# Per-head q and k transfers, a searched order of the engines, and last rows stored in two halves, in a fused attention and maxout-FFN kernel

## The chip, the core and the metric

The kernel runs on one NeuronCore of a Trainium2 chip. The core has five instruction queues that run side by side[...]: TensorE (PE in the profile; its weight loads are listed apart as PEld), VectorE (DVE), ScalarE (ACT), GpSimd (POOL) and SyncE (SP). Sixteen DMA engines move data between memory and the on-chip SBUF; a transfer is started by an instruction on POOL, SP or ACT. The metric is the device time of one execution in microseconds, taken as a median over runs.

## The reference

Batch 4, 8 heads, 768 positions, head width 64, in float32. Each query attends to the 128 latest positions and to the first 4 positions ("sinks"). The result goes through a feed-forward layer with three up-projections of which the largest value is kept:

```
scores = (q @ k.T) / sqrt(64)
keep   = (col < 4) | ((0 <= row - col) & (row - col < 128))
a      = softmax(where(keep, scores, -1e9))
x      = (a @ v)            # heads side by side: 3072 rows x 512
h      = max(x @ w1, x @ w2, x @ w3)      # 3072 x 768
out    = h @ w_out                        # 3072 x 512, float32
```

## The kernel before

**Tiling.** The 3072 rows are 24 tiles of 128. Two tiles make a chunk of 256 positions, three chunks make a batch, so chunks 0 to 11 cover the four batches. The eight heads are two groups (g = 0, 1) of four, and four heads lie on the four 32-partition quarters of a tile. One unit of attention is a chunk and a group: scores for four heads on PE (line 484), exponential on ACT (490), mask on DVE (498), product with v on PE (516, and 507 for the sinks), reciprocal and scaling on DVE (526, 535). The scaled rows are then turned so that features lie on partitions: in the first five blocks by PE and a copy on ACT (545, 565), from block 5 (`FIRST_BY_DMA`) on by a DMA transpose that SP issues (570).

**Blocks.** The feed-forward layer runs over blocks of two or four tiles, listed in `BLOCKS`: 2, 2, 2, 4, 4, 4, 4, 2 tiles. Per block there are 18 up-projection groups of four matmuls each (643, called H below, of 256 columns in a block of two tiles and 512 in one of four), evacuated by ACT (652) and by DVE with a running maximum (657), and for each tile one output group of six matmuls with the matrix `wo` (671, called Y), copied by ACT (678) and stored by SP (685). The attention of a later block runs beside the feed-forward work of an earlier one.

**Transfers.** q and k are loaded by POOL with a cast to bf16 (198): one transfer for q or k, a chunk and a group, over 128 partitions of 512 elements. v is loaded per tile over all heads (204), the three up-projection matrices in nine transfers of two column blocks each (209: w0, w2, w4 below, three transfers each), and `wo` in one (310). Only the very first q, and the first k of group 1, come in float32 on SP and ACT (188) and are cast by ACT (349); the first k of group 0 comes on POOL. The chunk's q and k are then transposed on DVE (345). POOL may have eight loads under way: each waits for the one eight places before it, and POOL's loads are kept in the order in which they are listed: first k, v of chunk 0, q and k of chunk 1, v of chunk 1, w0, w2, w4, q and k of chunk 2, its v, `wo`, then chunk by chunk. The cast buffers of q and k hold eight chunks, so chunk 8 waits until chunk 0's have been transposed.

**Order.** No engine chooses its order at run time. The program builds a list of tasks, each with an engine, a cost in microseconds, what it depends on, and a due time `want`; `arrange` plays them through a model of the engines, the PSUM and SBUF rings and one DMA server (0.38 MB per us, 0.2 for v), and at each step takes what can start first, with ties going to the earlier `want`. The order in which it took them is the order in each engine's queue. An instruction whose input is late holds up everything behind it on its engine.

Of the kernel before, what the change touches and what calls it, by code (L numbers as in the profile page):

```python
# [40 lines left out]
def arrange(tasks):  # L41


    engines = {}
    for n, t in enumerate(tasks):
        t.n = n
        engines.setdefault(t.eng, []).append(t)
    for q in engines.values():
        q.sort(key=lambda t: (t.want, t.n))
    clock = dict.fromkeys(engines, 0.8)  # L50
    order = []
    slack = 0.03
    while any(engines.values()):
        best = None
        for e, q in engines.items():
            pick = None
            for t in q[:200]:
                if any(d.end is None for d in t.deps):
                    continue
                at = clock[e]  # L60
                for d in t.deps:
                    at = max(at, d.end + (d.lat if d.eng != e else 0.0))
                frees = [r.free_at() for r in t.alloc]
                if None in frees:
                    continue
                at = max([at] + frees)
                if pick is None or at < pick[0] - slack:
                    pick = (at, t)
            if pick and (best is None or pick[0] < best[0]):
                best = pick  # L70
        if best is None:
            for e, q in engines.items():
                for t in q[:8]:
                    print(e, t.name, [d.name for d in t.deps if d.end is None],
                          [(r.nm, [u.name for u in r.taken[-r.n].users[r] if u.end is None]) for r in t.alloc if r.free_at() is None])
        assert best is not None
        at, t = best
        t.start, t.end = at, at + t.cost
        clock[t.eng] = t.end
        for r in t.alloc:  # L80
            r.taken.append(t)
        engines[t.eng].remove(t)
        order.append(t)
    return order
# [3 lines left out]
def kernel(  # L88
# [51 lines left out]
    for nm, g in (("q", 0), ("q", 1), ("k", 1)):  # L140
        first[nm, g] = const.tile([128, 512], F32, name=f"{nm}_f{g}")
# [12 lines left out]
    lanes, lanes_i = [], []  # L154
# [3 lines left out]
    def load(name, mb, want, f, eng="POOL", cost=0.75, deps=(), lat=1.3):  # L158
        t = task(eng, cost, f, deps=deps, want=want, name="i" + name)
        if eng == "POOL":  # L160
            if len(lanes) >= 8:
                t.deps.append(lanes[-8])
            t.deps += lanes_i[-1:]
            lanes_i.append(t)
        dma_done[name] = task("DMA", mb / (0.2 if name[0] == "v" else rate), lambda: None, deps=[t], want=want, lat=lat, name=name)
        if eng == "POOL":
            lanes.append(dma_done[name])
        return dma_done[name]
# [8 lines left out]

    def raw(nm, ch, g):
        if (nm, ch, g) not in raws:
            raws[nm, ch, g] = io.tile([128, 512], BF16, name=f"{nm}_raw{g}", tag=f"{nm}_raw{g}", bufs=NBUF)  # L180
        return raws[nm, ch, g]
# [14 lines left out]
    def qk_chunk(nm, src, ch, g):  # L196
        def f():
            nc.gpsimd.dma_start(out=raw(nm, ch, g), in_=rows(src, ch, g))  # L198
        return f
# [14 lines left out]
    for g in range(NQ):  # L214
        load(f"q0.{g}a", 0.13, -2000 + g, qk_first("q", q, g, nc.sync, (0, 1)), eng="SP", cost=1.0)
        load(f"q0.{g}b", 0.13, -2000 + g, qk_first("q", q, g, nc.scalar, (2, 3)), eng="ACT", cost=0.95)
    load("k0.1a", 0.26, -1998, qk_first("k", k, 1, nc.sync), eng="SP", cost=2.2)


    rank = [-1000.0]  # L220

    def nxt():
        rank[0] += 1
        return rank[0]
# [3 lines left out]
    def qk_loads(ch, g):  # L228
        for nm, src in (("q", q), ("k", k)):
            deps = [tr_done[nm, ch - NBUF, g]] if ch >= NBUF else []  # L230
            load(f"{nm}{ch}.{g}", 0.26, nxt(), qk_chunk(nm, src, ch, g), deps=deps, lat=3.0)
# [61 lines left out]
    load("k0.0", 0.26, nxt(), qk_first("k", k, 0, nc.gpsimd), cost=2.2)  # L293
    for _ in range(3):
        lanes.append(lanes[-1])
    t_own = task("POOL", 1.8, make_own, want=nxt(), name="own")
    t_ident = task("POOL", 0.6, make_ident, want=nxt(), name="ident")
    v_loads(0)
    for g in range(NQ):
        qk_loads(1, g)  # L300
    v_loads(1)
    w_loads(0)
    t_bd = task("POOL", 0.6, make_bd, want=nxt(), name="bd")
    t_sel = task("POOL", 0.8, make_sel, deps=[t_bd], want=nxt(), name="sel")
    w_loads(2)
    w_loads(4)
    for g in range(NQ):
        qk_loads(2, g)
# [17 lines left out]
    t_mask = task("DVE", 0.9, make_masks, deps=[t_own], want=-999, name="mask")  # L326
    t_neg = task("DVE", 0.4, make_negs, deps=[t_mask], want=-998, name="neg") if N_BY_PE else None
# [5 lines left out]
    def transposes(ch, g, wants):  # L333

        for nm, want in zip("qk", wants):
            def f(nm=nm):
                src = raw(nm, ch, g).bitcast(F32)
                dst = tile_T(nm, ch, g).rearrange("p s e -> p (s e)").bitcast(F32)
                if nm == "q" and ch < FIRST_PLAIN:
                    dst = dst.rearrange("p (s j m) -> p j s m", s=2, j=8)  # L340
                    src = src.rearrange("p (j s m) -> p j s m", j=8, s=2)
                else:
                    dst = dst.rearrange("p (m j) -> p j m", j=8)
                    src = src.rearrange("p (j c) -> p j c", j=8)
                nc.vector.transpose(dst, src)  # L345
            deps = [dma_done[f"{nm}{ch}.{g}{x}"] for x in ("", "a", "b") if f"{nm}{ch}.{g}{x}" in dma_done]
            if ch == 0 and (nm, g) in first:
                def cast(nm=nm):
                    nc.scalar.copy(raw(nm, 0, g), first[nm, g])
                deps = [task("ACT", 0.6, cast, deps=deps, want=want,  # L350
                             name=f"cast{nm}{g}")]
            if ch >= NBUF:
                deps += [s_done[ch - NBUF, g]]
                deps += [s_done[ch - NBUF + 1, g]] if ch - NBUF + 1 < ch else []
                if (ch - NBUF) % NC:
                    deps.append(es_done[divmod(ch - NBUF, NC)])
            tr_done[nm, ch, g] = task("DVE", 0.46 if nm == "q" and ch < FIRST_PLAIN else 0.63, f, deps=deps, want=want, name=f"tr{nm}{ch}.{g}")
# [88 lines left out]
    def unit(ch, g, tts, blk, off, w0, dw):  # L446
# [120 lines left out]
        def xt_dma(tt):  # L567
# [18 lines left out]
            tt: task("DVE", 0.1 + n_e[tt] / 1880, masks(tt), deps=[es[tt], t_mask if ch < FIRST_PLAIN else t_plain],  # L586
# [35 lines left out]
        cp = task("ACT", 0.08 + 0.26 * len(tts), xt_copy, deps=xps, want=w0 + 4.5 * dw, name=f"XC{nm}")  # L622
# [6 lines left out]
    def block(blk, tok0, ntok, w0, length):  # L629
# [36 lines left out]
        def ygroup(m):  # L666
            def f():
                ps = ps_h.tile([128, 512], F32, name="y", tag="h")
                box["y", m] = ps
                for fb in range(FSUB):  # L670
                    nc.tensor.matmul(ps, lhsT=box["h"][:, fb, 128 * m:128 * m + 128],  # L671
                                     rhs=wo_sb[:, fb, :], start=(fb == 0), stop=(fb == FSUB - 1))
            return f

        def yout(m):
            def f():
                y_sb = ffn.tile([128, 512], F32, name="y_sb", tag="y_sb", bufs=4)
                nc.scalar.copy(y_sb, box["y", m])  # L678
                box["ysb", m] = y_sb
            return f  # L680

        def store(m):
            def f():
                r = tok0 + 128 * m
                nc.sync.dma_start(out=out[r:r + 128, :], in_=box["ysb", m])
            return f

        n = 0
        for fb in range(FSUB):
# [26 lines left out]
            h_last[fb] = prev  # L716
        for m in range(ntok // 128):
            want = w0 + n * step
            n += 1
            p = task("PE", 1.31, ygroup(m), deps=list(h_last.values()) + [dma_done["wo"]], want=want,  # L720
                     lat=0.2, alloc=[h_ring], name=f"Y{blk}.{m}")
            d = task("ACT", 0.6, yout(m), deps=[p], want=want + step, alloc=[y_ring], name=f"YC{blk}.{m}")
            i = task("SP", 0.7, store(m), deps=[d], want=want + 2 * step, lat=2.5, name=f"YO{blk}.{m}")
            d.users[y_ring] = [i]
            p.users[h_ring] = [d]
            y_all.setdefault(blk, []).append(p)
# [12 lines left out]
    def prepare(ch, base, per):  # L739
# [5 lines left out]
        if ch >= NC:  # L745
            for g in range(NQ):
                qk_loads(ch, g)
            v_loads(ch)
# [30 lines left out]
BLOCKS = [[0, 1], [2, 3], [4, 5], [6, 7, 8, 9], [10, 11, 12, 13], [14, 15, 16, 17], [18, 19, 20, 21], [22, 23]]  # L779
# [41 lines left out]
```

## Time and profile before

| what | before |
| --- | --- |
| median of 11 runs | 189.65 us (188.93 to 190.15) |
| the profiled execution: time, span | 188.47 us, 186.7 us |
| PE busy, share of the span | 166.5 us, 89% |
| DVE busy | 130.1 us, 70% |
| ACT busy | 92.8 us, 50% |
| POOL busy (its transfers' issue included) | 66.1 us, 35% |
| DMA packets of POOL's queue: share of 16 engines' span | 75.6% |
| memory read, written | 25.17 MB, 6.29 MB |

The span runs from the first to the last of the program's own instructions; the profiled execution's time is 1.77 us longer than its span. A matmul that waits for its input inside a run of matmuls counts as busy PE, so PE's share hides part of its stalls. The granted PE clock was 1.00 throughout. Idle time of an engine that nothing waits for costs nothing. In a row of the stage view each engine has its busy microseconds and, in brackets, the number of instructions.

### The profile page before, as it was taken

The page shows a single profiled execution, that of the slowest core. Times are in us where ns is not written, and L with a number is a line of the kernel's source. Part 1 is how long each engine was busy: PE and PEld are TensorE (multiplying, and loading weights), DVE is VectorE, ACT ScalarE, POOL GpSimd, SP SyncE. Part 2 cuts the span into 40 slices and gives each one's busy share as a digit, 9 for nine tenths or more (in the row PEclk, how much of TensorE's full clock was granted, in tenths as well). Part 3 has the DMA queues.
Part 4 walks back from the last instruction along what each step waited for, and adds up shares of the span by engine and source line. Part 5 has one row for each costly group of instructions (what it writes and reads, how often), then busy time and mean ns, then how long its engine had stood idle before and what let it go on. Part 6 is the DMA issues. An engine that isn't in the chain of part 4 may idle for free.

```text
span 186.7 us, 4368 instructions
## 1 busy us (share of the span) xinstructions
PE 166.5 (89%) x1700; PEld 100.0 (54%) x1720; DVE 130.1 (70%) x307; ACT 92.8 (50%) x162; POOL 66.1 (35%) x102
## 2 busy tenths in 40 slices
PE   0266997969999899999999999999999999999991
PEld 0133696738777664555554455544456444554870
DVE  6568468757989998989997868706599456570550
ACT  4545832764837673556656165554553662213421
POOL 7968995736575739755610000000000000000000
PEclk9999999999999999999999999999999999999999
DMA  6989999999999999999998001170031440005302
GB/s 147 103 100 176 196 196 169 198 158 144 196 110 129 218 113 98 142 201 136 108 117 244 1 20 39 31 245 9 0 38 23 113 173 0 0 4 145 136 0 112
DMA packets 63796, 20.95 MB, mean 112 GB/s; under 512 B 49184, under 2 KB 60320, under 8 KB 63776
## 3 DMA queue, kind: packets, MB, share of 16 engines
q0 software_dynamic: 53920, 12.26, 75.6%
q1 hardware_dynamic: 9664, 8.16, 14.7%
q8 instruction: 13, 0.21, 0.5%
q10 hardware_dynamic: 192, 0.26, 0.4%
q14 instruction: 7, 0.06, 0.1%
HBM read 25.17 MB, written 6.29 MB: 168 GB/s over the span
## 4 chain that ended last, share of the span: by engine, by line
PE 70%; DMA 10%; POOL 10%; DVE 4%; issue 2%; ACT 2%; DVEq 0%; ACTq 0%; POOLq 0%
PE h L643 42%; PE y L671 17%; DMA wo_sb<-in_moe_w_out_dram 6%; PE o L516 4%; PE st L484 4%; DMA q_raw<-in_q_dram 4%; POOL w_sb L209 3%; POOL v_sb L204 2%; DVE h_sb L657 2%; PE o L507 2%; POOL k_raw L188 1%; DVE x L535 1%; PE xt L545 1%; POOL q_raw L198 1%; POOL k_raw L198 1%
## 5 line engine op out<-in xcount | busy, mean ns | idle before, releaser
L643 PE MATMUL h<-xT,w_sb 128*128 128x256 bf16 (+1 forms) x564 | 103.9, 328 | 1.0
L657 DVE TENSOR_TENSOR h_sb<-h,h_sb 128x256 bf16<-128x256 f32 (+1 forms) x96 | 53.1, 555 | 30.7 <-PE h L643 18.3
L643 PEld LDWEIGHTS <-w_sb 128*128 128x128 bf16 x576 | 53.6, 99 | 33.3 <-issue 1.5
L490 ACT ACTIVATE e_sb<-st 128x1024 bf16<-128x1024 f32 (+1 forms) x48 | 44.5, 962 | 17.1 <-PE st L484 14.4
L652 ACT CAST h_sb<-h 128x256 bf16<-128x256 f32 (+1 forms) x48 | 23.2, 484 | 42.9 <-PE h L643 42.9
L671 PE MATMUL y<-wo_sb,h_sb 128*128 128x512 bf16 x136 | 32.0, 379 | 1.9 <-DMA wo_sb<-in_moe_w_out_dram 1.5
L204 POOL DMA_DIRECT2D v_sb<-in_v_dram x24 | 21.8, 909 | 6.2 <-DMA q_raw<-in_q_dram 4.4
L678 ACT COPY y_sb<-y 128x512 f32<-128x512 f32 x24 | 14.1, 586 | 18.2 <-PE y L671 16.3
L484 PE MATMUL st<-qT,kT 32*128 32x128 bf16 (+1 forms) x512 | 16.1, 253 | 7.5 <-DVE kT L345 7.3
L671 PEld LDWEIGHTS <-h_sb 128*128 128x128 bf16 x144 | 13.6, 97 | 17.2 <-DMA wo_sb<-in_moe_w_out_dram 1.7
L516 PE MATMUL o<-v_sb,e_sb 128*128 128x65 bf16 x352 | 19.1, 197 | 2.5 <-DVE e_sb L498 1.4
L516 PEld LDWEIGHTS <-e_sb 128*128 128x128 bf16 x352 | 17.1, 99 | 7.6 <-DVE e_sb L498 2.5
L498 DVE TENSOR_TENSOR e_sb<-e_sb,mask 128x1024 bf16<-128x1024 bf16 (+1 forms) x28 | 17.2, 625 | 5.1 <-ACT e_sb L490 5.1
L198 POOL DMA_DIRECT2D k_raw<-in_k_dram x22 | 15.1, 684 | 10.7 <-DMA wo_sb<-in_moe_w_out_dram 3.2
L484 PEld LDWEIGHTS <-kT 32*128 32x128 bf16 x512 | 10.4, 97 | 14.1 <-DVE kT L345 7.8
L198 POOL DMA_DIRECT2D q_raw<-in_q_dram x22 | 15.3, 697 | 7.1 <-DMA v_sb<-in_v_dram 3.2
L498 DVE TENSOR_TENSOR e_sb<-e_sb,plain 128x1024 bf16<-128x1024 bf16 (+1 forms) x20 | 13.2, 658 | 6.5 <-ACT e_sb L490 6.4
L345 DVE STREAM_TRANSPOSE kT<-k_raw 128x256 f32<-128x256 f32 x24 | 14.7, 627 | 1.9 <-DMA k_raw<-in_k_dram 1.6
L565 ACT COPY xT<-xt 128x256 bf16<-128x256 bf16 x28 | 9.1, 386 | 8.5 <-PE xt L545 8.5
L345 DVE STREAM_TRANSPOSE qT<-q_raw 128x256 f32<-128x256 f32 x24 | 12.1, 510 | 0.9 <-DMA q_raw<-in_q_dram 0.9
L535 DVE TENSOR_TENSOR x<-o,rc 128x256 bf16<-128x256 f32 x28 | 11.9, 425 | 1.0
L526 DVE RECIPROCAL rc<-o 128x4 f32<-128x4 f32 x48 | 8.3, 173 | 2.3 <-PE o L516 2.3
(47 smaller groups left out, 63.7 us busy)
## 6 DMA issues: line engine op xcount, KB each, us to landing
out_dram<-y_sb SPq DMA_DIRECT2D x24, 256.0 KB
v_sb<-in_v_dram POOLq DMA_DIRECT2D x24, 128.0 KB, 8.8
q_raw<-in_q_dram POOLq DMA_DIRECT2D x22, 128.0 KB, 8.9
k_raw<-in_k_dram POOLq DMA_DIRECT2D x22, 128.0 KB, 8.2
w_sb<-in_moe_w_dram POOLq DMA_DIRECT2D x9, 256.0 KB, 7.2
wo_sb<-in_moe_w_out_dram POOLq DMA_DIRECT2D x1, 768.0 KB, 11.6
vbd<-v_sb SPq DMA_DIRECT2D x48, 0.5 KB
q_f<-in_q_dram ACTq DMA_DIRECT2D x4, 64.0 KB
```

What stands on the lines that cost most here:

```text
L198: nc.gpsimd.dma_start(out=raw(nm, ch, g), in_=rows(src, ch, g))
L204: nc.gpsimd.dma_start(out=vbufs[b][:, :, n, :D], in_=s[:, n])
L345: nc.vector.transpose(dst, src)
L484: nc.tensor.matmul(ps[:, i, col:col + n], lhsT=kk[r, k0:k0 + 128, e], rhs=qT[r, q0:q0 + n, e], start=(e == 0 and not by_pe), stop=(e == 1) ...
L490: nc.scalar.activation(st["e"][:, :, cols(tt)], st["ps"][:, :, cols(tt)], AF.Exp, scale=scale)
L498: nc.vector.tensor_tensor(out=ee, in0=ee, in1=m.unsqueeze(1).to_broadcast(list(ee.shape)), op=ALU.mult)
L516: nc.tensor.matmul(o[:, i, :], lhsT=st["e"][:, i, col:col + 128], rhs=vbufs[b][:, 4 * g + i, kb, :], start=(c == 0 and n == 0), stop=(n == ...
L643: nc.tensor.matmul(ps[:, :ntok], lhsT=w_sb[:, wi, d, fb * 128:fb * 128 + 128], rhs=xTs[blk][:, d, :ntok], start=(d == 0), stop=(d == DSUB ...
L652: nc.scalar.copy(hs, ps[:, :ntok])
L657: nc.vector.tensor_tensor(out=hs, in0=ps[:, :ntok], in1=hs, op=ALU.max)
L671: nc.tensor.matmul(ps, lhsT=box["h"][:, fb, 128 * m:128 * m + 128], rhs=wo_sb[:, fb, :], start=(fb == 0), stop=(fb == FSUB - 1))
L678: nc.scalar.copy(y_sb, box["y", m])
```

## The change

- **q and k by head.** `qk_head` takes the place of `qk_chunk`: one transfer brings one head's q or k for a whole batch into a 32-partition quarter of a tile `raw_b` of three chunks. In batch 0 it brings chunks 1 and 2 alone, since chunk 0 still comes through `qk_first`. The buffers hold all four batches, and no load of q or k waits for a buffer any more. Of the first k, heads 0 and 1 of each group come on POOL in bf16, heads 2 and 3 on SP in float32, cast by ACT.
- **POOL's list.** In place of chunk-by-chunk loads: first k, v of chunk 0, w0, q and k of batch 0 group 0, then group 1, v of chunk 1, w2, w4, v of chunk 2, `wo`; later q and k batch by batch with v of the batch's first chunk between the two groups. POOL's loads are no longer tied to their listed order; the eight lanes become a ring of the model.
- **A searched order.** `run_model` is the old `arrange`, made faster. `vary` shifts the due times of some tasks in a window of time, drawn from a seed; `arrange` applies 140 listed seeds one after the other and uses the last order. The model's costs for the mask and for the copy of turned rows are changed slightly.
- **Blocks.** 2, 2, 2, 2, 4, 4, 4, 4 tiles in place of 2, 2, 2, 4, 4, 4, 4, 2. Block 5, from which rows are turned by DMA, now begins at tile 12 (before at 14), and the plain masks and q layout begin at chunk 6 (before at 7).
- **The end.** In the last block the first five of a tile's six output matmuls are a task apart from the sixth. The last tile's output is computed in two halves of 256 columns: the first copied by ACT and stored by SP, the second copied by DVE and stored by ACT.

```diff
-    def qk_chunk(nm, src, ch, g):
+    def qk_head(nm, src, b, h, c0):
         def f():
-            nc.gpsimd.dma_start(out=raw(nm, ch, g), in_=rows(src, ch, g))
+            g, i = divmod(h, 4)
+            nc.gpsimd.dma_start(
+                out=raw_b(nm, b, g)[32 * i:32 * i + 32, c0:],
+                in_=src[b, h].rearrange("(c p j) d -> p c (j d)", p=32, j=8)[:, c0:])
         return f
...
+    def raw_b(nm, b, g):
+        if (nm, b, g) not in raws:
+            raws[nm, b, g] = io.tile([128, NC, 512], BF16, name=f"{nm}_raw{g}", tag=f"{nm}_raw{g}", bufs=B)
+        return raws[nm, b, g]
...
         if eng == "POOL":
-            if len(lanes) >= 8:
-                t.deps.append(lanes[-8])
-            t.deps += lanes_i[-1:]
+            t.alloc = [lane_ring]
+            t.users[lane_ring] = [d]
...
-        load(f"q0.{g}a", 0.13, -2000 + g, qk_first("q", q, g, nc.sync, (0, 1)), eng="SP", cost=1.0)
+        load(f"q0.{g}a", 0.13, -2000 + g, qk_first("q", q, g, nc.sync, (0, 1)), eng="SP", cost=1.1)
         load(f"q0.{g}b", 0.13, -2000 + g, qk_first("q", q, g, nc.scalar, (2, 3)), eng="ACT", cost=0.95)
-    load("k0.1a", 0.26, -1998, qk_first("k", k, 1, nc.sync), eng="SP", cost=2.2)
+        load(f"k0.{g}a", 0.13, -2000 + g, qk_first("k", k, g, nc.sync, (2, 3)), eng="SP", cost=1.1)
...
     v_loads(0)
-    for g in range(NQ):
-        qk_loads(1, g)
-    v_loads(1)
     w_loads(0)
+    qk_loads(0, 0, 1)
     t_bd = task("POOL", 0.6, make_bd, want=nxt(), name="bd")
     t_sel = task("POOL", 0.8, make_sel, deps=[t_bd], want=nxt(), name="sel")
+    qk_loads(0, 1, 1)
+    v_loads(1)
     w_loads(2)
     w_loads(4)
-    for g in range(NQ):
-        qk_loads(2, g)
     v_loads(2)
...
+    for seed in SEEDS:
+        wants = vary(wants, tasks, seed)
+        order = run_model(tasks, wants)
     return order
...
+            halves = ((0, 256, "ACT"), (256, 512, "DVE")) if last and m == ntok // 128 - 1 else ((0, 512, "ACT"),)
...
-BLOCKS = [[0, 1], [2, 3], [4, 5], [6, 7, 8, 9], [10, 11, 12, 13], [14, 15, 16, 17], [18, 19, 20, 21], [22, 23]]
+BLOCKS = [[0, 1], [2, 3], [4, 5], [6, 7], [8, 9, 10, 11], [12, 13, 14, 15], [16, 17, 18, 19], [20, 21, 22, 23]]
```

## The prediction

> **What bounds the kernel now.** I read the page's slices first, then busy time by stage, then the chain of waits, then the order of single instructions in the first 40 us. Of the stage view these are the rows that I use:
>
> ```profile
> 7.04:19.79 12.75, 8.37 (x129) 4.78 (x129) 8.74 (x22) 7.65 (x15) 10.54 (x19) 1.00 1.36 134
> 19.79:39.91 20.12, 17.51 (x208) 13.57 (x204) 13.69 (x34) 10.48 (x23) 14.16 (x23) 1.00 1.46 187
> 39.91:70.77 30.86, 29.40 (x378) 21.71 (x382) 26.72 (x75) 18.75 (x38) 19.62 (x27) 1.00 1.80 151
> 70.77:183.08 112.31, 111.20 (x991) 59.91 (x1006) 76.72 (x165) 52.46 (x84) 16.00 (x21) 1.00 0.56 83
> 183.08:186.70 3.62, 0.00 (x0) 0.00 (x0) 0.00 (x0) 0.58 (x1) 0.00 (x0) 1.00 0.38 145
> ```
>
> The columns after the length are PE, PEld, DVE, ACT, POOL, clock, DMA. From 70.77 us, where block 3's H begins, PE is full. Busy time flatters PE, so I price its work by the dense stretches of the chain of waits: four H matmuls 0.44 us at 256 columns and 0.86 at 512; a Y matmul 0.217; a unit's 24 score matmuls 0.57, its 16 in a batch's first chunk 0.45; eight PV matmuls 0.25; one for the sinks 0.11; two turning matmuls 0.11. With the counts of each stage this gives dense work of 18.9 us up to 39.9, 28.5 from there to 70.8, and 111.9 in the 112.3 us after. So PE loses 21.0, 2.4 and 0.4 us; the tail is 3.6. Only the first 71 us and the tail have anything to give.
>
> ```profile
> 14.17 0.43 DVE L345 STREAM_TRANSPOSE qT<-q_raw 128x256 f32<-128x256 f32 x1
> 16.16 0.64 DVE L345 STREAM_TRANSPOSE kT<-k_raw 128x256 f32<-128x256 f32 x1 [0.64 <-DMA k_raw<-in_k_dram]
> 17.25 0.17 DVE L526 RECIPROCAL rc<-o 128x4 f32<-128x4 f32 x1
> 19.79 7.66 PE L643 MATMUL h<-xT,w_sb 128*128 128x256 bf16 x52
> 28.27 0.82 POOL L310 DMA_DIRECT2D wo_sb<-in_moe_w_out_dram x1 [0.27 <-DMA w_sb<-in_moe_w_dram]
> 39.91 2.27 PEld L671 LDWEIGHTS <-h_sb 128*128 128x128 bf16 x12 [1.69 <-DMA wo_sb<-in_moe_w_out_dram]
> ```
>
> The first H starts at 19.79: the last normalization of block 0 (17.25) stands on DVE behind transposes of chunk 1, one of which waits for its load. Its 52 matmuls then take 7.66 us instead of 5.7, in step with the weights, whose transfers land from 18.66 to 29.36 us, the last six 1.34 apart. Y of block 0 waits for `wo`, landed at 39.87. The head is therefore bound by transfers and by the order of their uses; from 40 to 70 DVE, 26.7 of 30.9 us busy, feeds a block of four tiles to a PE that has only blocks of two to work on.
>
> [...] here the first k quarters took 2.8 to 3.3 us from issue to landing. Their issue was the limit there, so this trace shows no sustained rate of quarter transfers.
>
> **The change, part by part.**
>
> *q and k by head.* The transfer now:
>
> ```profile
> L198 POOL DMA_DIRECT2D k_raw<-in_k_dram x22 | 15.1, 684 | 10.7 <-DMA wo_sb<-in_moe_w_out_dram 3.2 <-DMA v_sb<-in_v_dram 2.6 <-DMA q_raw<-in_q_dram 2.5
> L188 POOL DMA_DIRECT2D k_raw<-in_k_dram x4 | 2.1, 540 | 0.8 <-POOLq L802 0.8
> ```
>
> 128 rows cost POOL 0.69 us, 32 rows 0.54; by a line through both, a head's 96 rows cost 0.64 and batch 0's 64 rows 0.59. 44 transfers at 0.69 (30.4 us) become 16 at 0.59 and 48 at 0.64 (40.2): POOL +9.8 us, 66 to 76 of the 100 us in which it loads. Data time: a weight transfer of 524 KB per 1.34 us is 391 KB/us, so a chunk's q (262 KB) costs 0.67 and a head (197 KB) 0.50 at the same rate; the four q/k and two v transfers of a chunk land every 6.77 us (`wo` to the last, 60.9 us for nine), so v costs 2.04. Equal rate means no change, 12 x 0.67 = 16 x 0.50 = 8.0 us a batch. [...] Bounds: 0.45 (slight gain) to 1.0 (twice[...]). I take 0.52.
>
> *Order of data.* Chunk 2's q and k no longer follow w4. w0 now follows v of chunk 0 (landed 11.84) directly: three transfers, 15.9 instead of 21.3. But w2 and w4 have chunk 2's 2.7 us ahead of them: last weights near 32 instead of 29.4. In front of `wo` stands the same volume as before, hence 40. H can start near 16; until w2 this is worth only two column blocks, 6 x 0.44 = 2.6 us. After 32, two column blocks of blocks 0 and 1 are left, 5.3 us, which fits before 40. So by 40 PE could have done H of blocks 0 and 1 (36 x 0.44 = 15.8) and all attention of batch 0 (7.5): 23.3 against 18.9, at most -4.4. Chunk 1's q, k now land behind w0 and its attention moves into the H work; and an order searched on a model whose v costs 1.3 us where the trace has 2.04 won't fit exactly. I take 60%: -2.6.
>
> *First scores.* SP issues heads 2, 3 of k group 0 right after q group 0, ending 2.6 us; cast 0.62 and transpose 0.64 on top of a 2.4 us landing give scores at 6.3 instead of 7.0. q group 1 moves back 0.85 us on SP; ACT has one cast more, 0.6. PV of the second tile waited for v (11.88) anyway and covers all three; without that cover they would give -0.7. Counted 0.
>
> *Blocks.* Dense H and Y work is the same, four blocks of each size. Y of block 2 may be followed by H of block 3 once chunk 3 alone is through, where before chunks 3 and 4 had to be. That takes the DVE cause of the 2.4 us away. What is late next: chunk 3 now needs 16 head transfers and two of v. At 0.52 and 2.04 behind `wo` that is 40 + 8.3 + 4.1 = 52.4 us for group 1, before 43.4. Its chain (transposes 1.1, scores 0.5, exponential 1.0, mask 0.7, PV 0.25, normalization 0.6, turn and copy 1.0, queueing 1.5) ends at 59. PE meanwhile, with everything before 40 done, has two Y pairs, H of block 2, a third pair and chunk 3: 7.8 + 7.9 + 2.6 = 18.3, until 58.3. With the 60% above it has 60. So between 0 and 3 us lost; I take 2.0 for 2.4: -0.4. Chunks 4 and 5 are then there with chunk 3, and v at 2.04 each keeps ahead of them. At the end DVE idles through 20.6 us of last block instead of 10.4; it has 121.7 us to do by 162, which leaves slack.
>
> *DMA turning from tile 12.* Four turned unit halves less on PE: 8 x 0.055 = 0.44, and four ACT copies of 0.386. SP issues two transposes more, 2.4 us, where it waits; chunk 6's q transposes rise from 0.44 to 0.63 on DVE, 0.4 us in slack. -0.4.
>
> *Buffers.* POOL's waits for a chunk's transposes (2.3 us) and the like go; they lay after 70 us, where nothing waits for POOL. 0; 48 KB of partition space instead of 32.
>
> *End.* PE's last matmul, ACT copy 0.58, then 3.0 us of store. The second half's DVE copy should take the 0.42 of a 256-column evacuation, and ACT's queue issues the store while SP issues the other; half the bytes may save 0.1. Bounds 0 to -0.5: -0.3. Splitting Y into five and one changes the order alone: Y already started while DVE was still on the last H.
>
> *The remaining order.* After 70 us 0.4 us is left to gain, but a searched order can also lose there: DVE and ACT stand in queues whose model costs are approximate. I take 0, bounds -0.4 and +2.
>
> Sum: -2.6 - 0.4 - 0.4 - 0.3 = -3.7. On the profiled execution's 188.47 (span 186.7 and 1.77 around it) this is 184.8; the median of the runs shown is 1.18 above, so **186.0**.
>
> **Rivals.** *The head fills up.* The order serves weights so well that the 4.4 us and the whole 2.4 come, with 0.4 + 0.3: -7.5, 182.1. For it: the idle time is there, and DVE was 67% busy in those 40 us. Against it: `wo` and chunk 3 come no sooner. *Chunk 3 gives it back.* The batch-wide loads make PE wait the full 3 us at chunk 3, and w2, w4 come later still: -2.6 + 0.6 + 2.0 - 0.7 = -0.7, 189.0, near no change. For it: the 9 us later landing. *Slower: quarter transfers at a lower rate.* Each 0.1 us more on a head's transfer puts 16 x 0.067 = 1.1 us in front of `wo` and 16 x 0.1 = 1.6 more in front of chunk 3, where PE already waits: 2.7 us in all. So the gain of 3.7 is gone at 0.66 us a head; halfway to the upper bound, 0.76, it is 6.4 - 3.7 = +2.7, 192.3; at the bound of 1.0, 12.8 - 3.7 = +9.1, 198.8. For it: [...] POOL's issue at 0.64, which is above 0.52 and bites where the queue runs dry[...]. *That it does not do what it says* is open only for the searched order, whose result the diff does not show; the transfers and blocks are fixed.
>
> **How the numbers follow.** Likeliest 0.50 (own range 184 to 188.3), fuller head 0.20 (180.5 to 184), given back 0.12 (188 to 190), slower 0.18 (190 to 198.8). Range 181.0 to 191.8 leaves out about 0.17. A measurement of this kernel can tell about 0.2%, 0.4 us. Faster 0.74 (0.49 of the likeliest, 0.20, 0.05 of given back), within 0.2% 0.06, slower 0.20.
>
> **What would show it.** First H near 16 us; last weight near 32 and Y at 40; at 40 us PE's dense work near 21.5; H of block 3 near 60; from there to the last matmul no more than 1 us lost; 24 PE-turned tile halves instead of 28; last store issued 0.4 us after its matmul. POOL near 76 us busy. It is wrong if `wo` lands after 43, if the first uses of batch 1 wait for q or k for more than 3 us, or if DVE waits in the middle of the run.

## The result, and the profile after

The changed kernel takes **187.13 us** (median of 12 runs, 185.59 to 188.57) against 189.65 for the kernel before (47 runs beside it): ratio **0.9872, 95% interval 0.9846 to 0.9897**. Forecast were 186.0 us, 181.0 to 191.8. The profiled execution took 187.3 us with a span of 185.6; before it was 188.47 and 186.7. Some executions of a program are over 1.5% slower than its fastest (here 188.57 us against 185.59), so the ratios leave these out, and the one profile of such an execution (194.32 us, of the run with large and small loads mixed) is read for its order only.

The stage view of the kernel after, cut at the same times as before; the last cut is its own last matmul. After the length come PE, PEld, DVE, ACT, POOL, the clock, the DMA share and GB/s:

```profile
0.00:7.04 7.04, 0.00 (x0) 0.00 (x0) 2.94 (x8) 2.00 (x3) 5.78 (x16) 1.00 0.87 147
7.04:19.79 12.75, 5.67 (x94) 3.90 (x94) 7.83 (x25) 7.05 (x13) 11.74 (x25) 1.00 1.11 136
19.79:39.91 20.12, 18.58 (x251) 14.74 (x242) 15.29 (x37) 13.00 (x25) 15.01 (x25) 1.00 1.42 169
39.91:70.77 30.86, 29.47 (x364) 21.86 (x366) 25.71 (x68) 17.69 (x36) 25.99 (x39) 1.00 1.43 174
70.77:181.80 111.03, 110.21 (x1008) 59.63 (x1020) 79.73 (x173) 51.76 (x83) 13.24 (x21) 1.00 0.45 82
181.80:185.60 3.80, 0.00 (x0) 0.00 (x0) 0.32 (x1) 0.37 (x1) 0.00 (x0) 0.84 0.38 138
```

Until 19.79 us PE does less than before (5.67 busy instead of 8.37), from there to 39.91 more (18.58 instead of 17.51). What moved in the head of the kernel (its first 40 us; not to be mixed up with a head of the attention) shows in the order of single instructions of the kernel after (start, length, engine, and in brackets the idle time before it and what ended it):

```profile
1.30 1.64 POOL L268 DMA_DIRECT2D w_sb<-in_moe_w_dram  x2 [0.80 <-POOLq L901]
2.91 2.02 POOL L243 DMA_DIRECT2D k_raw<-in_k_dram  x4
...
10.63 0.64 DVE L402 STREAM_TRANSPOSE kT<-k_raw 128x256 f32<-128x256 f32 x1 [5.47 <-DMA k_raw<-in_k_dram]
...
11.32 0.83 PE L546 MATMUL st<-qT,kT 32*128 32x256 bf16 x16 [11.32 <-DVE mask L315]
...
21.84 2.38 PE L705 MATMUL h<-xT,w_sb 128*128 128x256 bf16 x11
...
37.76 3.11 PE L705 MATMUL h<-xT,w_sb 128*128 128x256 bf16 x27
...
40.38 0.56 POOL L255 DMA_DIRECT2D k_raw<-in_k_dram  x1 [3.52 <-DMA wo_sb<-in_moe_w_out_dram]
...
42.74 1.46 PE L733 MATMUL y<-wo_sb,h_sb 128*128 128x512 bf16 x5
...
68.19 1.48 PE L705 MATMUL h<-xT,w_sb 128*128 128x256 bf16 x12
```

The searched order puts two weight transfers on POOL ahead of the first k. The k then lands between 9.59 and 10.50 us (before 4.23 to 6.22), DVE waits 5.47 us for it, and the first scores start at 11.32 (before 7.04), the first H at 21.84 (before 19.79). The last weight lands at 35.46 (before 29.36). `wo` lands at 40.10 (before 39.87), yet nothing on PE waits for it now: before, the Y of block 0 did, 1.5 us. The H of block 3 starts at 68.19. The two H rows show one thing more: 11 matmuls in 2.38 us at 21.84, 27 in 3.11 us at 37.76, which is 0.216 and 0.115 each for the same shape (more on it in the last section).

Because a start time says little about the whole, I use the prediction's prices again (H 0.11 a matmul at 256 columns, Y 0.217 and so on), count each stage's weight loads in the trace, and call what is left of the stage "lost". Both kernels were profiled a second time in the runs at the end of the study; the second value is from those profiles. All times in us:

| PE lost in | before | after |
| --- | --- | --- |
| 0 to 40 | 20.8 / 20.6 | 21.0 / 19.6 |
| 40 to 80 | 2.7 / 4.1 | 2.5 / 3.0 |
| 80 to 160 | 1.9 / 1.3 | 0.9 / 0.7 |
| span | 186.7 / 187.6 | 185.6 / 184.6 |

In the mean of the two profiles of each kernel the head gives 0.4 us, 40 to 80 gives 0.65, 80 to 160 gives 0.8. The turning matmuls that are gone give 0.44 at the prices (24 turned tile halves instead of 28, eight unit halves at 0.055). The sum is 2.3; the mean spans (187.15 and 185.1) differ by 2.05, the medians by 2.5. Two profiles of one kernel differ by up to 1.4 us in a stage, more than any of these differences, so the split by stages is not resolved; what it does show is that no single stage holds the gain. The head, for which I had counted 2.6, has at most 1.2 in any pairing of the profiles, and in the first pair nothing.

### The profile page after: what moved, and what is told of

Same layout as the page of the kernel before. It is cut to its first block, busy times and chain, and to the rows that moved or that the text cites. A ratio compares the mean times of both kernels' runs of the same rounds, so it can differ in the third digit from the quotient of the medians.

```text
span 185.6 us, 4386 instructions
## 1 busy us (share of the span) xinstructions
PE 163.9 (88%) x1700; PEld 100.1 (54%) x1718; DVE 131.8 (71%) x308; ACT 91.9 (50%) x159; POOL 71.8 (39%) x122
## 4 chain that ended last, share of the span: by engine, by line
PE 63%; POOL 16%; DMA 15%; issue 3%; DVE 1%; ACT 0%; DVEq 0%; ACTq 0%; POOLq 0%
PE h L705 38%; PE y L733 14%; DMA v_sb<-in_v_dram 6%; DMA wo_sb<-in_moe_w_out_dram 5%; PE o L578 4%; PE st L546 4%; POOL k_raw L255 4%; POOL q_raw L255 4%; DMA w_sb<-in_moe_w_dram 4%; POOL v_sb L263 3%; POOL w_sb L268 3%; PE o L569 2%; PE xt L607 1%; DVE h_sb L719 1%; POOL sel L350 1%
## 5 line engine op out<-in xcount | busy, mean ns | idle before, releaser
L705 PE MATMUL h<-xT,w_sb 128*128 128x256 bf16 (+1 forms) x566 | 100.8, 327 | 1.5 <-DVE h_sb L719 0.8
L705 PEld LDWEIGHTS <-w_sb 128*128 128x128 bf16 x576 | 54.3, 99 | 37.0 <-issue 1.4
L719 DVE TENSOR_TENSOR h_sb<-h,h_sb 128x256 bf16<-128x256 f32 (+1 forms) x96 | 52.8, 555 | 24.8 <-PE h L705 19.4
L733 PE MATMUL y<-wo_sb,h_sb 128*128 128x512 bf16 (+1 forms) x142 | 32.8, 370 | 0.4
L743 ACT COPY y_sb<-y 128x512 f32<-128x512 f32 (+1 forms) x24 | 13.8, 584 | 18.2 <-PE y L733 14.2
L255 POOL DMA_DIRECT2D k_raw<-in_k_dram x32 | 17.7, 557 | 9.2 <-DMA v_sb<-in_v_dram 3.8
L255 POOL DMA_DIRECT2D q_raw<-in_q_dram x32 | 17.6, 555 | 3.6 <-DMA w_sb<-in_moe_w_dram 1.5
L560 DVE TENSOR_TENSOR e_sb<-e_sb,plain 128x1024 bf16<-128x1024 bf16 (+1 forms) x24 | 15.1, 640 | 1.3 <-ACT e_sb L552 1.2
L560 DVE TENSOR_TENSOR e_sb<-e_sb,mask 128x1024 bf16<-128x1024 bf16 (+1 forms) x24 | 15.0, 641 | 1.2 <-ACT e_sb L552 1.1
L597 DVE TENSOR_TENSOR xd<-o,rc 128x256 bf16<-128x256 f32 x24 | 10.2, 425 | 0.8
L597 DVE TENSOR_TENSOR x<-o,rc 128x256 bf16<-128x256 f32 x24 | 10.2, 425 | 0.8
```

What stands on the lines that cost most here:

```text
L255: nc.gpsimd.dma_start(out=raw_b(nm, b, g)[32 * i:32 * i + 32, c0:], in_=src[b, h].rearrange("(c p j) d -> p c (j d)", p=32, j=8)[:, c0:])
L560: nc.vector.tensor_tensor(out=ee, in0=ee, in1=m.unsqueeze(1).to_broadcast(list(ee.shape)), op=ALU.mult)
L597: nc.vector.tensor_tensor(out=x, in0=o[:, :, :D], in1=rc.unsqueeze(2).to_broadcast([128, 4, D]), op=ALU.mult)
L705: nc.tensor.matmul(ps[:, :ntok], lhsT=w_sb[:, wi, d, fb * 128:fb * 128 + 128], rhs=xTs[blk][:, d, :ntok], start=(d == 0), stop=(d == DSUB ...
L719: nc.vector.tensor_tensor(out=hs, in0=ps[:, :ntok], in1=hs, op=ALU.max)
L733: nc.tensor.matmul(box["y", m, lo][:, lo:hi], lhsT=box["h"][:, fb, 128 * m:128 * m + 128], rhs=wo_sb[:, fb, lo:hi], start=(fb == 0), stop= ...
```

## The experiments

Theories at the start. **A, the prediction's:** the order of data in the first 40 us gives the time; where the trace after lacks it, the late first k has eaten it. **B:** the first 40 us are worth little either way, and what gains is the searched order of the engines, on whatever loads and blocks. Ratios are to the kernel before on the same chip, with 95% intervals.

### The first k ahead of the weights

```diff
+    ks = sorted([t for t in order if t.name in ("ik0.0", "ik0.1")], key=lambda t: t.name)
+    order = [t for t in order if t not in ks]
+    at = min(n for n, t in enumerate(order) if t.name.startswith("iw"))
+    order[at:at] = ks
```

> The changed kernel with one edit: on POOL the four transfers of the first k stand ahead of the two weight transfers that the searched order had put before them (group 0 first); every other queue keeps its order. Theory A (the missing head gain is the first k landing at 9.6 to 10.5 us instead of 4.2 to 6.2): k lands by 6 us, the first scores start near 7 instead of 11.3, the first H near 18 instead of 21.8, and 1.5 to 3 us of it reach the end: 184.0 to 185.6 us. Rival B (the head is bound by the last weights at 35.5 us and wo at 40.1, which do not move): the first scores move just as far, but the time stays at 186.7 to 187.5.

Measured 187.39 us, 0.9892 [0.9849, 0.9936]: no different from the change itself. PE's instructions in order of time, of this kernel:

```profile
6.61 0.83 PE L546 MATMUL st<-qT,kT 32*128 32x256 bf16 x16 [6.61 <-DVE kT L402]
11.80 0.83 PE L546 MATMUL st<-qT,kT 32*128 32x256 bf16 x16 [4.37 <-ACT e_sb L552]
...
20.56 1.04 PE L481 MATMUL sk<-qT,kbd 128*32 128x256 bf16 x14 [0.50 <-DVE qT L402]
21.53 2.74 PE L705 MATMUL h<-xT,w_sb 128*128 128x256 bf16 x12
```

The first scores come 4.7 us sooner, and PE waits for the second ones instead, because ACT's queue stands in the old order: the cast of the second k, whose load comes later, is ahead of the first exponential there. The first H moves by 0.3 us: in PE's queue it stands behind the sink scores of a later chunk (L481, 20.56), which wait for that chunk's q. The late first k is a real loss at its place and costs nothing at the end that these runs resolve. A falls in the form "late k ate the gain".

### Blocks alone

The kernel before with the new `BLOCKS` line and nothing else (turning by DMA from tile 12 comes with it).

> The kernel before with the new list of blocks alone (2,2,2,2,4,4,4,4), its own planner, loads and end. Theory A (the blocks carry the gain: PE gets a block of two tiles where it had to wait for four, and 0.44 us of turning less): 187.0 to 188.5, H of block 3 before 68 us. Rival B (the blocks give only the 0.4 us of turning and the rest comes from loads and search): 189.0 to 189.8. Rival C (without the search they cost, since the last attention must be ready 10 us earlier): above 190.

Measured 190.67 us, 1.0038 [1.0007, 1.0069]: slightly slower. Lost are 20.0 us up to 40, 4.35 from 40 to 80 and 1.6 after, instead of 2.7 and 1.9 between 40 and 160 in the profile before. The first H of block 3 does start sooner, at 64.78 instead of 70.39, but the stall that a smaller block 3 was to remove comes back later, 1.9 us between 70 and 80 where before lost 0.1.

### The change without its search

```diff
-SEEDS = (
-    50012, 50017, 50019, ...
+SEEDS = ()
```

> The changed kernel with the list of seeds empty, so that the order is the planner's first one; loads by head, blocks and end stay. Theory A (the search carries the gain): 189 to 191. Rival B (loads and blocks carry it, and the search only spoiled the head by its weight transfers): 184.5 to 187, with first scores near 7 us and no wait of PE above 2 us between 40 and 70 us.

Measured 192.87 us, 1.0159 [1.0098, 1.022]. All new transfers, blocks, model costs and the new end, in the order that the model takes from the due times as written, are **slower than before by 1.6%**. (The list that is emptied here has 144 seeds, not the 140 given further up.) The stage view of this kernel:

```profile
0.00:40.00 40.00, 23.45 (x324) 16.11 (x325) 25.13 (x68) 20.51 (x38) 32.59 (x63) 1.00 1.16 146
40.00:80.00 40.00, 38.17 (x458) 28.46 (x458) 32.44 (x86) 23.05 (x46) 29.27 (x46) 1.00 1.40 169
80.00:160.00 80.00, 78.98 (x782) 41.98 (x793) 61.97 (x140) 40.52 (x62) 9.65 (x14) 1.00 0.43 77
```

and of the kernel before in the first two stages:

```profile
0.00:40.00 40.00, 25.97 (x333) 18.45 (x334) 26.71 (x69) 21.06 (x40) 30.47 (x55) 1.00 1.29 161
40.00:80.00 40.00, 38.49 (x459) 26.33 (x464) 34.91 (x92) 22.94 (x44) 27.24 (x36) 1.00 1.68 144
```

At the prices 23.4 us are lost up to 40, 2.6 and 2.8 more than in the two profiles of the kernel before; 4.0 up to 80 and 2.1 up to 160 lie within 0.2 of the larger of its two values. The search takes 5.7 us off this structure by the medians (192.87 to 187.13) and 5.4 by the ratios, more than twice the whole gain of the change.

### Chunk transfers in the changed kernel's order

Each place of a head's transfer now issues the chunk transfer of before, or nothing where there is none; all engines keep the order after. The same data is loaded.

```diff
-            nc.gpsimd.dma_start(
-                out=raw_b(nm, b, g)[32 * i:32 * i + 32, c0:],
-                in_=src[b, h].rearrange("(c p j) d -> p c (j d)", p=32, j=8)[:, c0:])
+            if i + c0 < NC:
+                nc.gpsimd.dma_start(out=raw(nm, NC * b + c0 + i, g), in_=rows(src, NC * b + c0 + i, g))
```

> The changed kernel with its order, but after chunk 0 the four head transfers of a q or k group are replaced by the transfers by chunk over 128 partitions (three for a batch, two in batch 0), issued from the same places. Theory A (a head transfer is no cheaper in data time, 0.51 us for 197 KB): all loads end at 95 plus or minus 2 us, and the time stays within 0.6 us of the changed kernel. Rival B (the chunk transfers with their extra small packets, 384 more of 4 bytes each than a head transfer has, are what made loading slow): loads end at 99 us or later, wo lands at 41 or later, and the time rises by 0.7 to 3 us.

Measured 191.56 us, 1.0065 [1.0027, 1.0102]. The last load lands at 97.24 (after 95.14) and `wo` at 39.03, so the loads are slowed by less than the rival said, and the time by more. Lost are 21.6 up to 40 (about as after), 5.5 up to 80. The order of single instructions, of this kernel:

```profile
63.42 0.64 DVE L401 STREAM_TRANSPOSE qT<-q_raw 128x256 f32<-128x256 f32 x1 [3.85 <-DMA q_raw<-in_q_dram]
63.91 0.93 DVE L718 TENSOR_TENSOR h_sb<-h,h_sb 128x256 bf16<-128x256 f32 x2
...
64.36 0.60 PE L704 MATMUL h<-xT,w_sb 128*128 128x256 bf16 x4 [3.07 <-DVE h_sb L718]
```

DVE stands 3.85 us at a transpose whose q isn't there; the maximum of the feed-forward layer is queued behind it, and PE, whose H needs the PSUM buffer that this maximum frees, waits 3.07. So this order needs what the per-head loads bring in time (4.4 us by the medians, 3.7 by the ratios). It doesn't show that they are better as such: this order was searched for them.

### The old structure with a search of its own

Loads, blocks, costs and end of before; only `run_model`, `vary` and the loop over seeds are taken from the change, with 255 seeds kept out of 23,500 drawn, each because the model's last store (plus a tenth of PE's mean end) came sooner. Without seeds `run_model` puts the tasks of the old program in the same order on every engine as `arrange` did, so a difference is due to the seeds and not to the rewritten model.

```diff
+    for seed in SEEDS:
+        wants = vary(wants, tasks, seed)
+        order = run_model(tasks, wants)
     return order
```

> The kernel before, with its own loads by chunk, blocks, model costs and end, but its order drawn by the change's search: the same two functions, 255 seeds of 23,500 tried, kept when the model's last store or a tenth of the mean end of PE's tasks came earlier. In the planner's own model the last store moves from 187.7 to 181.8 us (in the change from 190.5 to 180.8). Theory A (the gain is the search's and needs none of the other parts): 185.5 to 187.5 us. Rival B (the search pays only together with loads by head, since chunk loads arrive late): within 0.6 us of the kernel before, or slower.

Measured 186.14 us, **0.9815 [0.9771, 0.986]**. The stage view of this kernel:

```profile
0.00:20.00 20.00, 9.20 (x144) 6.07 (x145) 13.48 (x37) 11.93 (x21) 18.29 (x36) 1.00 1.16 141
20.00:40.00 20.00, 15.84 (x178) 12.62 (x176) 11.81 (x30) 7.93 (x18) 12.31 (x20) 1.00 1.59 176
40.00:70.77 30.77, 30.45 (x440) 21.96 (x438) 28.63 (x79) 21.30 (x42) 19.02 (x26) 1.00 1.91 150
```

From 40 to 70.77 PE and DVE are fuller here than in the first profile of either kernel, and 1.5 us are lost between 40 and 80. (A second profile, below, shows another place.) None of the new transfers, blocks or halves is needed for the gain. B holds.

### Large and small loads mixed

On top of the first experiment's edit, each two of batch 0's head transfers are followed by one of w2, w4 or v, so that the weights come sooner in POOL's queue; the other engines keep their order.

> The changed kernel with the first k in front of the weights, and with POOL's sixteen head transfers of batch 0 no longer in one row: after every two of them stands one of the ten large transfers (w2, w4, v of chunks 1 and 2). Theory A (the head is late because sixteen short transfers in a row, 0.53 us of issue for 0.34 us of data, let the DMA engines run dry between 12 and 22 us): the last weight lands near 32 instead of 35.5 us, wo near 37 instead of 40, DMA moves over 140 GB/s in 14 to 23 us instead of 78 to 99, and the time falls by 0.5 to 2 us, to 185 to 186.6. Rival B (PE's fixed queue, with the sink scores of chunks 1 and 2 ahead of the first H, wastes it): weights and wo land earlier but the first H is no earlier than 21 us and the time is within 0.5 us of the changed kernel, or slower because those sink scores wait for later heads.

Measured 192.45 us, 1.012 [1.0066, 1.0173]. The waits of PE up to 45 us, of this kernel (total, times, longest):

```profile
PE st L546 <- DVE kT L402: 9.3, 2, 6.8
PE st L546 <- DVE rc L588: 4.5, 1, 4.5
PE st L546 <- ACT e_sb L552: 3.0, 1, 3.0
```

The last weight lands 2 us sooner (33.50), `wo` at 40.31 as ever, the first H at 27.94, 6 us later: the attention of chunks 1 and 2 stands ahead of it on PE and waits for its q and k. Here the order of the loads mattered through what stands first in the queues of the engines, not through when the weights were complete.

### The last tile in one piece

The changed kernel with all six output matmuls of the last tile at 512 columns, one ACT copy and one store.

> The changed kernel, same order, with the last tile's output in one piece: six matmuls of 512 columns, one ACT copy, one store by SP. Theory A (the halves give the 0.3 us of the prediction): 0.2 to 0.4 us slower. Rival B (two stores on two queues and the half copies give nothing, since the fixed time of a store, 3.0 us, ends the kernel): within 0.15 us. In the span after PE's last matmul: 3.8 us now; 3.6 for B, 4.1 for A.

Measured 187.85 us, 0.9897 [0.9847, 0.9947], not to be told from the change; the interval, half a per cent either way, could not show the forecast 0.2 to 0.4 us, so the tail has to. The instructions at the end of the changed kernel:

```profile
181.69 0.42 DVE L745 COPY y_sb<-y 128x256 f32<-128x256 f32 x1 [4.39 <-DMA out_dram<-y_sb]
181.85 0.37 ACT L743 COPY y_sb<-y 128x256 f32<-128x256 f32 x1 [0.72 <-PE y L733]
182.15 0.39 ACTq L751 DMA_DIRECT2D out_dram<-y_sb  x1
```

and of this one, whose span ends at 184.6:

```profile
175.82 5.13 PE L739 MATMUL y<-wo_sb,h_sb 128*128 128x512 bf16 x23
...
181.03 0.58 ACT L755 COPY y_sb<-y 128x512 f32<-128x512 f32 x1 [0.71 <-PE y L739]
```

From PE's end to the end of the span are 3.65 us in one piece (180.95 to 184.6) and 3.8 in halves (181.8 to 185.6). The copies are shorter, 0.37 to 0.42 instead of 0.58, but two stores are issued after them, and the rest of the tail does not shrink with the bytes: from the end of the last copy to the end of the span are 3.0 us in one piece and 3.4 in halves.

### New searches of the changed kernel

The model's DMA server is mended so that it serves transfers in the order of issue, as the trace does, where all 102 loads of POOL land in that order (the old model let the first k overtake a weight issued before it, which is how the late k came about); a few costs are set to the trace's; new seeds.

```diff
-            for x in q:
+            for x in sorted(q, key=lambda x: x[2])[:1] if e == "DMA" else q:
```

> The change with its model mended from the traces and searched anew: POOL's transfers served by the DMA in the order of their issue (in the change's model a later load with an earlier due time overtakes), issue 0.56 for a head and 0.93 for v, 1.6 us from data to landing, and costs of scores, PV, evacuations and the masks as measured; 188 seeds of 23,500 tried, its last store in the mended model 180.5 us. Theory A (what the search lost on the chip came from the model's errors): 183.5 to 186. Rival B (the rest of the loss is no error of these costs): 186 to 188, no better than the change.

> The changed kernel with the mended DMA model and a search from another range of seeds: all parts of the change stay, only the order differs. Theory A (any searched order of these loads and blocks ends at the same place, because what is lost in the head goes to loads that all of them share): ratio 0.984 to 0.989, PE lost before 40 us near 20. Theory B (the order that a search happens to find matters by a per cent): outside 0.982 to 0.992.

The first took 187.23 us, 0.986 [0.9822, 0.9898]; the second, the same edit with seeds from another range, 186.26, 0.9806 [0.9765, 0.9847]. PE's instructions in order of time, of the first, and below it its longest kind of wait up to 72 us after that of the first scores:

```profile
17.05 1.25 PE L705 MATMUL h<-xT,w_sb 128*128 128x256 bf16 x5
```

```profile
PE sk L481 <- DVE qT L402: 2.8, 2, 2.1
```

In the second row the sink scores wait for a transposed q: the early weights are paid for by q and k. The first H does start where I had forecast it, 4.8 us sooner than in the change, and 20.4 us are lost up to 40, within what two executions of one program differ by (21.0 and 19.6), 3.3 up to 80. In the trace its first 16 matmuls stand 0.213 us apart, until 20.4 us, and only then 0.109. The second search lost 19.6, 2.6 and 0.95 in the three stages. In its trace both starts are where the prediction had them, the first scores at 6.37 and the first H at 15.42, and yet only 1.0 to 1.2 us less are lost up to 40 than in the two profiles of the kernel before. An early first H was not worth what I had put on it.

### The changed kernel and the searched old structure side by side

> The changed kernel once more, on one chip beside the searched old structure. Theory A (the search carries the gain, and the old loads and blocks are as good a ground for it): ratio to before 0.987, and 0.3 to 0.6% above the searched old structure of the same call. Theory B (the two are the same, the earlier 0.6% was chance between chips): both within 0.2% of each other.

> The kernel before with a search of its own, the same program as in the earlier run, on one chip beside the changed kernel. Theory A: ratio to before 0.980 to 0.984, median near 186.1, below the changed kernel's of the same call. Theory B: 0.985 to 0.989, the same as the changed kernel.

On one chip, 186.93 us for the change (0.9838 [0.9797, 0.988]) and 186.95 for the searched old structure (0.9858 [0.9814, 0.9902]): the same. The 0.6% between their earlier ratios was not confirmed. The second profile of the searched old structure also moves the place of its gain: 18.9 us are lost up to 40 instead of 20.6, and 3.0 from 40 to 80 instead of 1.5; PE is busy for 29.10 us from 40 to 70.77 and not for 30.45, no more than before the search (29.31). So the search carries the gain, but which stretch of the order carries it these profiles do not show. Six programs from four searches and two structures (the change, the change with the first k moved or the last tile whole, the two new searches, the searched old structure) lie between 186.1 and 187.9; the unsearched ones lie at 189.65 (before), 190.67 (with the new blocks) and 192.87. Within that band I can name no best one: the second new search has the lowest ratio of the three measured side by side, and its interval overlaps the others.

### The kernel before, profiled again

> The kernel before, profiled a second time, because its profiled execution (188.47 us) lies 1.2 us under its median (189.65), while the changed kernel's (187.3) does not lie under its own (187.13): the two profiles differ by 1.2 us and the medians by 2.5. Theory A (the first profile fell on a quick execution, and the waits for chunk 3 and for DVE between 40 and 70 us vary from one execution to the next): profiled time 189 to 190.2, with 3 to 5 us of PE lost between 40 and 70 us instead of 2.6. Theory B (profiled executions of this order are quicker as a rule, and the waits are the same): 188.2 to 188.8 and 2.3 to 2.9 lost.

The profiled time was 189.26 us, and 4.1 us were lost from 40 to 80 instead of 2.7 (3.9 instead of 2.6 from 40 to 70). The page that I predicted from was of a quick execution, and its stalls between 40 and 70 us vary by more than a microsecond.

## Why the prediction was right, and where it was not

The time fell within the range and near the forecast, 187.13 for 186.0; the sum was -3.7, and -2.5 was measured. The steps behind it fared worse than the sum.

- **Order of data, -2.6: failed.** The first H was to start near 16 us and PE to have 21.5 us of dense work by 40. It started at 21.84, with 19.0 us (20.4 in the second profile) against 19.2 before (19.4). The step assumed that work which could be done earlier would be. Without the search the new order of data loses 2.6 us or more beyond the kernel before by 40, and where searches did bring the first H to 17.05 and 15.42, the work by 40 was 19.6 and 20.4. The reading under it was wrong too: the 7.66 us that the first 52 H matmuls of the kernel before took instead of 5.7 I had put down to the weights. In its trace the matmuls from 20.6 to 23.2 us stand 0.213 us apart, from 23.35 on 0.109: some 15 at about twice the time, 1.4 of the 1.96 us (one gap of 0.39 comes beside them). That is PE at half speed and not a wait for data: in the kernel after, the first ten stand 0.213 us apart too, and the weights that they use had landed by 13.51. Earlier weights alone would not have given it back. Rival "the head fills up" falls with it.
- **First scores at 6.3: wrong, and harmless.** They came at 11.32. I had not seen that a searched order may move the first k behind weights; moving it back changed nothing.
- **Transfers by head, "equal rate means no change": wrong in the good direction.** From `wo` to the last load nine chunks' loads took 55.0 us (40.10 to 95.14) instead of 60.9, 6.12 a chunk instead of 6.77; my 0.52 a head and 2.04 a v meant 6.85. (The 0.52 was my estimate, and no trace showed it; the weights' 391 KB/us give 0.50, and so 6.75.) With chunk transfers in the changed order it is 6.47, so about half of this is due to the form of the transfer; for the rest, order and buffers, there is no run of each alone. The slower rival, from 0.66 a head on (7.60 a chunk), for which the profile before had shown no rate either, is excluded. In the profile before nothing but POOL's own queue waited for loads after 70 us, so most of this lies in cover; in the changed order the loads before 65 us do matter, as the chunk transfers showed.
- **Blocks, -0.4 through block 3 near 60 us: failed as a mechanism.** H of block 3 started at 68.19. Blocks alone brought it to 64.78 and gave +0.4%. The 0.65 between 40 and 80 is within what two profiles of one kernel differ by there (2.7 and 4.1 before).
- **DMA turning, -0.4:** 24 turned halves as forecast, 0.44 at the prices; no run shows alone what this is worth in time.
- **End, -0.3: not there.** The tail was 3.8 us, before 3.62.
- **The remaining order, 0: the step that mattered most.** I took a searched order for a rearrangement that could gain 0.4 at most after 70 us. The 0.4 was itself a wrong sum: the weight loads of that stage in the trace before (286 H at 512 columns, 72 at 256, 108 Y and the attention) come to 110.2 us at the prices and not to 111.9, so 2.1 us were lost there. The search as a whole gave 5.4 to 5.7 us on the new structure and about 3 on the old. Where it gives them is open. Between 80 and 160 us the change lost 0.9 and 0.7 where before lost 1.9 and 1.3, but the searched old structure, just as fast, lost 1.4 there in both profiles; between 0 and 80 two profiles of one program differ too much.
- **POOL near 76 us busy:** 71.8. A head's 96 rows cost 0.56 us to issue and not 0.64; the line through 32 and 128 rows doesn't hold.

So the right time was luck: a gain from the order, which I had set to nothing, stood in for a gain in the first 40 us that did not occur.

## What to carry to other kernels

When a change brings new structure together with a new search over the order, run each alone: here the structure alone was 1.6% slower, the search alone on the old structure was as good as both. In queues of a fixed order a wait is worth what stands behind it: ending the first wait 4.7 us sooner moved the end by nothing that could be measured, while one late transpose on DVE cost PE 3.07 us. And profile the kernel before twice before a stall of two microseconds in it is given a cause.

## What the runs showed of the hardware

**The two forms of the transfer differ in their packets.** The queue of POOL's transfers (packets, MB, share of 16 engines' span), in the kernel before:

```profile
q0 software_dynamic: 53920, 12.26, 75.6%
```

and after, with the group of k's head transfers (busy, mean ns):

```profile
q0 software_dynamic: 37344, 12.20, 61.4%
...
L255 POOL DMA_DIRECT2D k_raw<-in_k_dram x32 | 17.7, 557 | 9.2 <-DMA v_sb<-in_v_dram 3.8
```

For nearly the same bytes there are 16,576 packets fewer, and the chunk transfers in the new order bring them back (53,920, 72.4%). They are packets of 4 bytes: 18,208 before, 1,632 after. The 1,632 are 16 for each of 102 transfers; before, 16 for each of 82 leave 16,896, which is 384 more for each of the 44 chunk transfers. With the form alone exchanged, the nine chunks behind `wo` took 58.2 us by chunk (39.03 to 97.24) and 55.0 by head, 6.47 and 6.12 a chunk; the 6.77 of the kernel before holds waits for buffers too (2.3 us of POOL for DVE's transposes). Which engine carried a packet the profile does not show, and what makes the extra packets was not shown. Four transfers over 32 partitions each were no slower here than the three over 128 in whose place they stand.

**PE ran at half speed up to 20 to 24 us, and again after a wait of 3.07 us.** The clock on the page is 1.00 through the whole first 40 us, and yet the H matmuls of 256 columns stand 0.213 us apart until 23.2 us before, 23.9 after, 20.4 in the first new search, and 0.109 afterwards. The first entry of the clock in each of these traces, 1.00, begins just there: at 23.27, 23.93 and 20.63. Ahead of it nothing is recorded, and the page's 1.00 there isn't to be trusted; the distance of the matmuls is the better witness. The order alone does not set the moment: in the first profile of the searched old structure the clock's entry begins at 20.16 and the first H at 20.12 already runs at 0.109, in the second, of the same program, it begins at 23.33 and 16 matmuls stand 0.213 apart. Part of what I call lost in the head is this (1.4 us among the H of the kernel before). The stage view of the run with chunk transfers, around its 3.07 us wait (61.29 to 64.36; the clock is the number after POOL's bracket), shows it with the clock recorded:

```profile
62.00:64.00 2.00, 0.00 (x0) 0.00 (x0) 0.58 (x2) 0.00 (x0) 1.29 (x2) 1.00 2.91 102
65.00:66.00 1.00, 0.87 (x16) 0.45 (x15) 0.90 (x3) 0.27 (x1) 1.00 (x2) 0.59 1.57 113
66.00:67.00 1.00, 1.00 (x24) 0.86 (x25) 0.93 (x5) 0.12 (x1) 0.59 (x1) 0.50 1.39 113
...
68.00:70.00 2.00, 1.95 (x19) 1.29 (x18) 1.46 (x4) 2.00 (x4) 1.57 (x3) 0.85 2.41 117
```

At the granted clock 0.41 and 0.5 us are missing in the slices from 65 and 66, 0.5 in the one left out (also at 0.50), 0.3 in the last: by this estimate about 1.7 of the 5.5 us that this run lost between 40 and 80 are not the wait but what came after it. The 24 score matmuls of a unit tie the two places together: 1.04 us at 66.67 in this run, at a recorded 0.50, and 0.64 at 57.93, at 1.00; in the kernel before they take 1.04 at 18.81, where no clock is recorded. What sets the moment of full speed was not shown: PE had broken work of the attention ahead of the H, and full speed came 3.5 us after the first H before, 2.1 after, 3.6 in the first new search. Nor does one wait of 3.07 us show how long a wait must be to end it. I had not counted half speed in the first 40 us.
